# A short convolution moved to TensorE, a filter transpose moved through DRAM, and a new load order, in a long-convolution and MLP kernel

## The chip, the cores and the metric

The kernel runs on one core of one Trainium2 chip. The metric is the device time of an execution in microseconds (us). Executions agree within about 1%. PE is TensorE, DVE is VectorE, ACT is ScalarE, POOL is GpSimd and SP is SyncE, which issues most of the transfers. The granted clock is the share of its full speed that PE was given, as the profile records it. The matmuls of this kernel write to buffers in PSUM; the copy of a result from there into SBUF, by ACT or DVE, is called an eviction here.

## The reference

All inputs are bf16. S = 2048 tokens, D = 512 channels, F = 1376, four taps in the short convolution.

```python
def _A_ref(q, k, v, shift_k, ssm_k, ssm_D):
    k_shift = sum(k_pad[:, t:t+S, :] * shift_k[:, ks-1-t] for t in range(4))   # short causal convolution
    kv = k_shift * v
    y = irfft(rfft(kv, 2*S) * rfft(ssm_k, 2*S))[:S] + kv * ssm_D               # long causal convolution
    return q * y
def _B_ref(x, w1, b1, w2, b2):
    return gelu(layernorm(x) @ w1 + b1) @ w2 + b2
x = A_q
x = x + _A_ref(layernorm(x), ...);  x = x + _B_ref(layernorm(x), ...)
x = x + _A_ref(layernorm(x), ...);  x = x + _B_ref(layernorm(x), ...)
```

(The text is shortened: casts and padding are left out, and the loop over taps is written as a sum.) Both A layers use the same k, v and filter, so y is the same in both. The kernel computes it once, in a first part, and then runs four groups of tokens twice through the MLP part.

## The kernel before

The long convolution is a transform in two stages of matmuls: stage 1 with table F, a transpose, stage 2 with table W, a product with the transformed filter, then the inverse with table M, a transpose, and the last stage with table G. Filter and data both go through stage 1 and a DVE transpose. The parts that the change touches:

```python
# loads: k and its 3-token halo, the filter on ACT's queue, v and the tables on SP's
nc.sync.dma_start(kh[:, KS - 1:, :], k_d.rearrange(TOK, p=P))
for p0, n in ((1, 112), (113, 15)):
    nc.scalar.dma_start(kh[p0:p0 + n, 0:h, :], ...)
for ct in range(CT):
    nc.scalar.dma_start(Kraw[:, ct, :], A_ssm_k[ct * P:(ct + 1) * P, :])
nc.sync.dma_start(uv[:], v_d.rearrange(TOK, p=P))
# ... cut ...
def kv_chunk(cc):                       # short convolution and product with v, on DVE, 128 channels
    nc.vector.tensor_tensor(m[:], kh[:, h:h + NT, c0:c0 + CW], sb(0), ALU.mult)
    for t in range(1, KS):
        nc.vector.tensor_tensor(m2[:], kh[:, h - t:h - t + NT, c0:c0 + CW], sb(t), ALU.mult)
        nc.vector.tensor_tensor(m[:], m[:], m2[:], ALU.add)
    nc.vector.tensor_tensor(uv[:, :, c0:c0 + CW], m[:], uv[:, :, c0:c0 + CW], ALU.mult)
# ... cut ...
def stage1(src, dst, cc, tag):          # for the filter (Ktok to ZK) and for the data (uv to ZX)
    for q in range(4):
        for i in range(8):
            nc.tensor.matmul(pz[:, i, :], Ft[:, q // 2, :], src[:, tau, c0:c0 + CW], start=True, stop=True)
        nc.scalar.activation(ZT[:, 8 * q:8 * q + 8, :], pz[:], AF.Copy)
    nc.vector.transpose(dst[...], ZT[...])          # as 32-bit pairs, 128x2048
# ... cut ...
k_transpose()
for cc in range(NCH):
    kv_chunk(cc)
    stage1(Ktok, ZK, cc, "pa")
    stage1(uv, ZX, cc, "pb")
```

After this come stage 2 of the filter (with swapped half copies made by DMA), the product loop (`x_mul`, `x_inv`), four bare transposes and the last stage. A layernorm of token group 0 is placed in the loop.

## Time and profile before

| | before |
|---|---|
| time, median of 4 runs | 340.0 us (339.73 to 340.84) |
| span of the profiled execution | 338.0 us |
| mean granted PE clock | 0.884 |
| DVE busy, PE busy | 225.2 us, 244.7 us |
| end of the first part (first DVE product of the output) | 158.66 us |

The prediction below shows the lines: the chain of work that ended last, the chain in order of time, the busy time by stretch, and the groups. A busy time is a sum over an engine and says nothing about order. The chain says which engine's work the next work waited for. The windows tell, for one stretch, how full each engine was; where one engine is nearly full, its work is the first candidate for what sets the length of the stretch.

### The profile page before, as it was taken

The page shows a single profiled execution, that of the slowest core. Times are in us where ns is not written, and L with a number is a line of the kernel's source. Part 1 is how long each engine was busy: PE and PEld are TensorE (multiplying, and loading weights), DVE is VectorE, ACT ScalarE, POOL GpSimd, SP SyncE. Part 2 cuts the span into 40 slices and gives each one's busy share as a digit, 9 for nine tenths or more (in the row PEclk, how much of TensorE's full clock was granted, in tenths as well). Part 3 has the DMA queues.
Part 4 walks back from the last instruction along what each step waited for, and adds up shares of the span by engine and source line. Part 5 has one row for each costly group of instructions (what it writes and reads, how often), then busy time and mean ns, then how long its engine had stood idle before and what let it go on. Part 6 is the DMA issues. An engine that isn't in the chain of part 4 may idle for free.

```text
span 338.0 us, 3487 instructions
## 1 busy us (share of the span) xinstructions
PE 244.7 (72%) x1312; PEld 122.5 (36%) x1312; DVE 225.2 (67%) x361; ACT 164.3 (49%) x206; POOL 19.8 (6%) x26
## 2 busy tenths in 40 slices
PE   0007546253786997107599999989999999999995
PEld 0007536153321322002235444444444444444442
DVE  2208999999534999894987988888787682020122
ACT  0106878055778887004667736246271653726300
POOL 3000000000010000001112112101011110000000
PEclk9999967555578999656969999999999999999999
DMA  7990000006599445000000000000000001010011
GB/s 229 374 390 4 2 0 2 0 0 249 186 234 222 106 167 167 0 0 0 2 0 1 2 0 0 2 0 1 3 0 0 2 0 50 14 45 17 18 62 47
DMA packets 7040, 21.94 MB, mean 65 GB/s; under 512 B 912, under 2 KB 4593, under 8 KB 5872
## 3 DMA queue, kind: packets, MB, share of 16 engines
q1 hardware_dynamic: 5890, 19.14, 18.1%
q10 hardware_dynamic: 1022, 2.59, 2.1%
q8 instruction: 10, 0.16, 0.2%
q0 software_dynamic: 112, 0.00, 0.1%
q14 instruction: 6, 0.05, 0.1%
HBM read 15.44 MB, written 2.10 MB: 52 GB/s over the span
## 4 chain that ended last, share of the span: by engine, by line
DVE 46%; PE 36%; DMA 8%; ACT 5%; POOL 3%; issue 2%; DVEq 0%; POOLq 0%; ACTq 0%
PE po L328 17%; PE ph L316 14%; DVE arena L200 9%; DMA arena<-in_A_ssm_k_dram 6%; DVE st L169 6%; DVE arena L266 5%; DVE kvm L159 4%; DVE kvt L158 4%; DVE arena L177 4%; ACT arena L207 3%; POOL rs L173 3%; DVE T L235 3%; DVE arena L244 3%; DVE T L234 2%; DMA arena<-in_A_k_dram 2%; DVE arena L297 2%
## 5 line engine op out<-in xcount | busy, mean ns | idle before, releaser
L328 PE MATMUL po<-arena 128*128 128x512 bf16 (+1 forms) x352 | 80.7, 379 | 1.3 <-DVE arena L331 1.3
L316 PE MATMUL ph<-arena 128*128 128x512 bf16 (+1 forms) x352 | 79.6, 387 | 0.7 <-ACT arena L308 0.7
L318 ACT ACTIVATE arena<-ph,B 128x512 bf16<-128x512 f32 (+1 forms) x88 | 60.2, 687 | 29.5 <-PE ph L316 29.5
L331 DVE TENSOR_TENSOR arena<-po,arena 128x512 bf16<-128x512 f32 x32 | 21.9, 683 | 50.1 <-PE po L328 50.1
L316 PEld LDWEIGHTS <-arena 128*128 128x128 bf16 (+1 forms) x352 | 35.9, 102 | 43.3 <-issue 3.9
L328 PEld LDWEIGHTS <-arena 128*128 128x128 bf16 (+1 forms) x352 | 33.8, 98 | 38.8 <-issue 1.4
L169 DVE BATCH_NORM_STATS2 st<-arena 128x6 f32<-128x512 bf16 x64 | 42.4, 676 | 5.2 <-DMA arena<-in_A_q_dram 4.5
L198 PE MATMUL pz<-arena,Ft 128*128 128x128 bf16 x256 | 25.8, 275 | 27.1 <-DVE arena L160 16.7
L199 ACT ACTIVATE ZT<-pz 128x1024 bf16<-128x1024 f32 x32 | 30.6, 1033 | 22.2 <-PE pz L198 21.7
L308 ACT ACTIVATE arena<-pt 128x512 bf16<-128x512 bf16 x32 | 17.3, 594 | 42.8 <-PE pt L307 42.5
L198 PEld LDWEIGHTS <-Ft 128*128 128x128 bf16 x256 | 22.6, 127 | 30.6 <-issue 26.3
L200 DVE STREAM_TRANSPOSE arena<-ZT 128x2048 f32<-128x2048 f32 x8 | 29.4, 3671 | 3.0 <-ACT ZT L199 3.0
L173 POOL TENSOR_TENSOR rs<-rs,mhalf 128x4 f32<-128x4 f32 x16 | 16.1, 1009 | 202.8 <-DVE rs L172 202.8
L187 PE MATMUL pk<-IDt,arena 128*128 128x128 bf16 x64 | 6.5, 285 | 26.9 <-DVE arena L143 26.6
L273 PE MATMUL py<-arena,Gt 128*128 128x512 bf16 x32 | 9.6, 452 | 17.9 <-DVE arena L266 17.6
L177 DVE TENSOR_SCALAR arena<-arena,rs,nm 128x512 bf16<-128x512 bf16 x64 | 22.1, 407 | 0.6
L242 PE MATMUL pv<-T,arena 128*128 128x512 bf16 x64 | 18.7, 393 | 3.0 <-DVE T L234 1.5
L274 ACT ACTIVATE arena<-py 128x1024 bf16<-128x1024 f32 x8 | 7.9, 1023 | 22.0 <-PE py L273 22.0
L232 ACT ACTIVATE xb<-px 128x1024 bf16<-128x1024 f32 x16 | 16.3, 1040 | 3.4 <-DVE T L235 3.3
L207 ACT ACTIVATE arena<-pk 128x1024 bf16<-128x1024 f32 x16 | 15.1, 1058 | 2.6 <-PE pk L206 2.6
L266 DVE STREAM_TRANSPOSE arena<-arena 128x2048 f32<-128x2048 f32 x4 | 16.2, 4121 | 0.1
L189 ACT ACTIVATE arena<-pk 128x2048 bf16<-128x2048 bf16 x4 | 7.3, 1874 | 18.4 <-PE pk L187 18.4
(38 smaller groups left out, 189.5 us busy)
## 6 DMA issues: line engine op xcount, KB each, us to landing
arena<-arena SPq DMA_DIRECT2D x8, 512.0 KB, 7.1
arena<-in_A_k_dram SPq DMA_DIRECT2D x1, 2048.0 KB, 12.5
arena<-in_A_ssm_k_dram ACTq DMA_DIRECT2D x4, 512.0 KB, 19.5
arena<-in_A_v_dram SPq DMA_DIRECT2D x1, 2048.0 KB, 12.8
arena<-tabM SPq DMA_DIRECT2D x1, 2048.0 KB, 7.6
arena<-in_A_q_dram SPq DMA_DIRECT2D x1, 2048.0 KB, 9.2
out_dram<-arena SPq DMA_DIRECT2D x16, 128.0 KB, 1.7
arena<-in_B_w_dram SPq DMA_DIRECT2D x1, 1376.0 KB, 5.9
```

The costliest lines, as they stand in the source:

```text
L169: nc.vector.bn_stats(st[:, i, :], x_t[:, GT * g + i, :])
L173: nc.gpsimd.tensor_tensor(rs[:], rs[:], mhalf[:], ALU.pow)
L177: nc.vector.tensor_scalar(out=dst[:, i, :], in0=x_t[:, GT * g + i, :], scalar1=rs[:, i:i + 1], scalar2=nm[:, i:i + 1], op0=ALU.mult, op1=A ...
L198: nc.tensor.matmul(pz[:, i, :], Ft[:, q // 2, :], src[:, tau, c0:c0 + CW], start=True, stop=True)
L199: nc.scalar.activation(ZT[:, 8 * q:8 * q + 8, :], pz[:], AF.Copy)
L200: nc.vector.transpose(dst[:, :, c0:c0 + CW].bitcast(F32).rearrange("p k c -> p c k"), ZT[:].bitcast(F32).rearrange("p b c -> p c b"))
L207: nc.scalar.activation(ZK[:, 2 * j:2 * j + 2, :], pk[:], AF.Copy)
L266: nc.vector.transpose(V2[:, :, c0:c0 + CW].bitcast(F32).rearrange("p k c -> p c k"), ZX[:, :, c0:c0 + CW].bitcast(F32).rearrange("p b c -> ...
L316: nc.tensor.matmul(ph[0:m, :], W1t[:, ct, ft * P:ft * P + m], lt[:, ct, :], start=ct == 0, stop=ct == CT - 1)
L318: nc.scalar.activation(ht[0:m, ft, :], ph[0:m, :], AF.Gelu_apprx_tanh, bias=B1[0:m, ft:ft + 1])
L328: nc.tensor.matmul(po[:], ht[0:m, ft, i * P:(i + 1) * P], W2t[0:m, ft, :], start=ft == 0, stop=ft == FT - 1)
L331: nc.vector.tensor_tensor(xs, po[:], xs, ALU.add)
```

## The change

The intent is to take work off DVE in the first part. The short convolution becomes matmuls with diagonal matrices, accumulated in PSUM over the four taps, so that DVE only multiplies by v. The filter's transpose after stage 1 goes to DRAM and back by DMA. The filter is loaded first. Evictions from PSUM are shared between ACT and DVE, PSUM buffers rotate over four instead of two and two, and the product loop lags by two steps instead of one. The core of the diff:

```diff
-    nc.sync.dma_start(kh[:, KS - 1:, :], k_d.rearrange(TOK, p=P))
     for ct in range(CT):
-        nc.scalar.dma_start(Kraw[:, ct, :], A_ssm_k[ct * P:(ct + 1) * P, :])
+        nc.sync.dma_start(Kraw[:, ct, :], A_ssm_k[ct * P:(ct + 1) * P, :])
+    for t4 in range(4):
+        nc.sync.dma_start(kn[:, 4 * t4:4 * t4 + 4, :], k_d.rearrange(TOK, p=P)[:, 4 * t4:4 * t4 + 4, :])
     nc.sync.dma_start(uv[:], v_d.rearrange(TOK, p=P))
 ... cut: tables, constants ...
+    for ct in range(CT):
+        for t in range(KS):
+            nc.gpsimd.tensor_scalar(out=DG[:, ct, t, :], in0=IDt[:], scalar1=sF[:, ct, t:t + 1], ...)
-    def kv_chunk(cc):        # 8 DVE instructions for each 128 channels
 ... cut ...
+        def k_filter_stage1(q):
+            for i2 in range(4):
+                for i in range(2):
+                    nc.tensor.matmul(pz[:, i, :], Ft[:, q // 2, :], Ktok[:, tau, :], start=True, stop=True)
+                evac(E_S1K[q][i2], ZT[:, 2 * i2:2 * i2 + 2, :], pz[:])
+            nc.sync.dma_start(apf(Zd, 8 * q * P * D, [[D, P], [P * D, 8], [1, D]]), ZT[:])
+        def kv_transpose(t4):     # k to channel-major, 16 PE transposes and one DVE copy
 ... cut ...
+        def kv(ct, o):
+            for i in range(8):
+                for t in range(KS):
+                    nc.tensor.matmul(pu[:, i, :], w, DG[:, ct, t, :], start=t == 0, stop=t == KS - 1)
+            nc.vector.tensor_tensor(us, pu[:], us, ALU.mult)
 ... cut ...
+        for q in range(4):
+            k_filter_stage1(q)
+            kv_transpose(q)
+        for k0 in range(0, NA, 8):
+            for g in range(4):
+                nc.sync.dma_start(ZK[32 * g:32 * g + 32, k0:k0 + 8, :],
+                                  apf(Zd, (32 * g + k0) * D, [[P * D, 32], [1, 8 * D]]))
+        for cc in range(4):
+            for o in range(2):
+                kv(cc, o)
+            if cc > 0:
+                stage1(cc - 1)
 ... cut: stage 2, the loop with a lag of two, the tail ...
```

## The prediction

(The text is cut, with marks, where it rested on figures that no trace or run of this case shows. The sums stand as they were: none of the terms of the 314 us is cut, but terms of three sums beside it are. In step (2) the 4.25 us for a quarter were chosen and not summed, and what DVE needs for its copies is cut beside them. The trip through DRAM came to 53 us; with the trace's numbers alone it is the same, as an estimate: 1 MB at 374 GB/s is 2.8 us, 4.2 MB are 11.2, each with the 1.7 us in which 128 KB landed: 35.5 + 17.4 = 52.9. In the cross-check the added work came to 29.2 us and the net to 25. In the trace before, the granted clock was 1.00 in the first of the two bursts and 0.50 in the second, and in the stretches it was 0.67, 0.84 and 0.94 with PE busy 35.9 of 65.8, 9.8 of 13.8 and 25.5 of 31.6 us.)

> **What bounds the kernel now.** I began with the page's chain that ended last, because a share of busy time averages over stages with different limits. Its first line splits the span by engine:
>
> ```profile
> DVE 46%; PE 36%; DMA 8%; ACT 5%; POOL 3%; issue 2%; DVEq 0%; POOLq 0%; ACTq 0%
> ```
>
> The same chain in order of time gives the stages. In these lines the columns are start, duration (us), what:
>
> ```profile
> 6.97 19.28 DMA arena<-in_A_ssm_k_dram
> 26.50 1.12 DVE kvt L158
> ...
> 95.94 10.19 ACT arena L207 x11
> ...
> 137.76 16.20 DVE arena L266 x4
> ...
> 158.66 1.24 DVE arena L297
> ```
>
> Nothing but loading happens until 26.5 us. From 26.5 to 92.3 the chain is VectorE alone (short convolution L155 to L160, transposes L200). From 92.3 to 106.1 it is mostly ScalarE evicting the filter's second stage. From 106.1 to 137.7 it is the VectorE-paced product loop, then 16.2 us of four bare transposes. The MLP part starts with L297 at 158.66. The diff touches nothing after that line, so I cut the run there and asked for the busy time of each engine by stretch:
>
> ```profile
> 0.00:26.50 26.50, 0.00 (x0) 0.00 (x0) 4.62 (x8) 1.28 (x1) 2.68 (x8) 1.00 0.89 318
> 26.50:92.30 65.80, 35.85 (x328) 29.77 (x329) 62.69 (x39) 41.34 (x40) 0.00 (x0) 0.67 0.15 52
> 92.30:106.10 13.80, 9.76 (x28) 3.19 (x28) 4.54 (x14) 11.41 (x14) 1.04 (x1) 0.84 0.93 239
> 106.10:137.70 31.60, 25.47 (x92) 8.33 (x92) 28.59 (x40) 23.59 (x25) 0.00 (x0) 0.94 0.52 143
> ```
>
> Columns: stretch, length, busy PE, PEld, DVE, ACT, POOL, granted clock, DMA share, GB/s. In the second row DVE is busy 62.7 of 65.8 us while DMA is used 15%: that row is what the change attacks. The costs come from the groups:
>
> ```profile
> L200 DVE STREAM_TRANSPOSE arena<-ZT 128x2048 f32<-128x2048 f32 x8 | 29.4, 3671 | 3.0 <-ACT ZT L199 3.0
> L159 DVE TENSOR_TENSOR kvm<-kvm,kvt 128x2048 bf16<-128x2048 bf16 x12 | 14.4, 1209 | 0.1
> L158 DVE TENSOR_TENSOR kvt<-arena,SK 128x2048 bf16<-128x2048 bf16 x12 | 14.2, 1213 | 0.0
> L244 DVE CAST arena<-pv 128x1024 bf16<-128x1024 f32 x8 | 9.8, 1219 | 0.9 <-PE pv L242 0.9
> L207 ACT ACTIVATE arena<-pk 128x1024 bf16<-128x1024 f32 x16 | 15.1, 1058 | 2.6 <-PE pk L206 2.6
> ```
>
> And two bursts of 128-column matmuls from the timeline show PE's two speeds, 61 ns each (1.95/32) and 110 ns each (4.42/40):
>
> ```profile
> 36.76 1.95 PE L198 MATMUL pz<-arena,Ft 128*128 128x128 bf16 x32 [2.05 <-DVE arena L160]
> 50.66 4.42 PE L198 MATMUL pz<-arena,Ft 128*128 128x128 bf16 x40 [1.56 <-DVE arena L160]
> ```
>
> [...]2048 elements in SBUF take 1.21 us, 1024 f32 elements from PSUM take 1.22. The trace has no DVE copy of bf16 from PSUM; [...]the stretch's granted clock of 0.67 goes with PE busy half the time. [...]the 32 KB identity on ACT's queue landed 12.7 us after its issue[...], and the filter[...] landed 17.9 to 20.5 us after issue. [...]the stores of 128 KB here landed in 1.7.
>
> **The change part by part.**
>
> (1) Load order. The filter (2.1 MB) is now first on SP's queue, ahead of k, v and the tables. The page shows 229 GB/s in the first slice (8.45 us, 1.9 MB) and 374 in the next. The remaining 0.3 MB then takes about 1 us, plus landing: 10.5 us instead of 26.5. A tiny add with D, whose load took until 9.3 us, precedes PE, and the b1 cast waited until 13.6 on the same in-order DVE. I choose PE's start at 12 us.
>
> (2) Filter path. 64 transposes took 6.5 us of PE; they stay, their evictions move to DVE[...], so PE is through at 18.5. Stage 1 becomes 32 matmuls of 512 columns, with 64 more transposes for k. Per quarter: PE 8 x 0.22 + 16 x 0.1 = 3.4 us, ACT 3 x 1.03 = 3.1[...]. Four rotating PSUM buffers make this a chain; I choose 4.25 per quarter, 17 in all: 35.5 us. The four filter transposes on DVE (4 x 3.67 = 14.7) are gone; 4.2 MB goes to DRAM and back instead. At the last quarter, [...]home at about 53 us.
>
> (3) Short convolution on PE. 28 TENSOR_TENSORs at 1.21 and one 1.23 copy leave DVE (35 us); four products (4.8) become eight from PSUM at 1.22 (9.8). PE gains 256 matmuls of 128 columns, beside 128 of stage 1: 384 x 0.061 = 23.4 us at full clock, 42 at half. DVE has 9.8 + 14.7 = 24.5, ACT 16 x 1.03 = 16.5. PE is dense from 12 us on, so I expect nearly full clock and PE and DVE to pace each other: 24.5 plus about 4.5 for the hand-overs of a 3.67 us transpose against 1.22 us products: 29 us, to 64.5.
>
> (4) Filter stage 2. It needs the DRAM data (53) and PSUM in rotation, so it starts at 64.5. ACT owes four evictions (4.1) and then 12 of 16 (12.4); DVE takes 4. That is 16 us: 80.5. The layernorm of group 0 fits in here, if q arrives: its buffer is free at 64.5, and 9.2 us from issue to landing gives 74.
>
> (5) Product loop. Same matmuls, same two products per step, same alternating evictions; only the lag is deeper. It is already 28.6 of 31.6 us DVE-busy, so I give it 31: 111.5.
>
> (6) Tail. Last transposes and the first output block: 158.66 - 137.7 = 21 us, unchanged: 132.5. The MLP then starts 158.66 - 132.5 = 26 us earlier. 340 - 26 = 314 us.
>
> A cross-check by DVE work: removed 35 + 4.8 + 14.7 = 54.5, added 9.8 (products)[...] + 9.8 (eight evictions) = 29.2; net 25 us. The earlier start adds 14 and the new hand-overs take back about as much.
>
> **The rivals.** First, PE becomes the bound of the convolution at the low clock. For: clock 0.67 in that stretch before, and 3.67 us transposes can stall PE. Against: PE has twice the work there. It would make (3) 42 to 45 us: 327 to 330. Second, the product loop waits for its table M or for q, both issued late on SP behind the eight half-swap copies. For: the diff places these loads after stage 2, where they were spread before. Against: in the trace before, q's load was issued at 87.54 although the code names it after the swaps, first issued at 92.55, so the order follows readiness; M's buffer is free at about 36. If it fails, about 8 to 12 us are lost: 322 to 326. Third, the DRAM round trip is slower than I think[...], and stage 2 waits. It has 11 us in hand, so it must take almost twice as long to cost anything; 317 to 320. Fourth, an upside: PE starts at 10.5, hand-overs are hidden, stage 2 is shared so well that ACT is free: 304 to 307.
>
> **Range and chances.** The sum is 314. The errors are mostly one-sided waits of up to 16 us and an upside of 10, and they are unlikely to come all together: 303 to 327. To be within 2% it would have to end above 333, which takes the low clock and a late load both; slower has no mechanism I can see, as at least 25 us of DVE work goes.
>
> **What would show it.** Right: first PE work at 10 to 14 us; filter stage 1 over by about 36; eight PSUM products of about 1.2 us[...] on DVE; granted clock above 0.85 from 36 to 65; stage 2's first matmul waiting on PSUM or ACT, not on DMA; the product loop still at about 3.5 us per two steps; the MLP stretch at 179 us, starting near 132. Wrong: [...]convolution matmuls at 110 ns; PE waiting for M or DVE for q after 80 us; stage 2 waiting on the reads from DRAM. If the MLP stretch itself changes, my cut at L297 was wrong.

## The result and the profile after

| | before | after |
|---|---|---|
| median | 340.49 us (16 runs, 338.9 to 341.33) | 309.65 us (11 runs, 308.67 to 311.49) |
| profiled span | 338.0 us | 306.8 us |
| mean granted PE clock | 0.884 | 0.939 |
| DVE busy, PE busy | 225.2, 244.7 us | 202.7, 248.8 us |
| end of the first part | 158.66 us | 127.11 us |

The ratio is 0.9098, with a 95% interval of 0.9078 to 0.9119. A ratio here is the mean time of one kernel's runs over that of the other's in the same rounds, so it is not quite the ratio of the medians that are quoted. The prediction was 314 us with 303 to 327: the time lies in the range, 4.3 us under the 314.

The chain that ended last, by engine, and then five pieces of the same chain in order of time (start, duration, what):

```profile
PE 43%; DVE 38%; DMA 5%; issue 5%; ACT 4%; POOL 3%; SPq 0%; DVEq 0%; ACTq 0%; POOLq 0%
```

```profile
2.13 8.47 DMA arena<-in_A_ssm_k_dram
...
30.57 6.54 PE p L227 x114
37.11 1.93 PE p L238 x32
...
42.15 4.19 DVE arena L240
...
127.11 1.24 DVE arena L370
```

DVE's share fell from 46% to 38% and PE's rose from 36% to 43%. Where before DVE stood in the chain from 26.5 to 92.3 us, all but alone (the chain has about 3 us of PE and ACT at 85.6), now PE's convolution (L227), PE's stage 1 (L238) and DVE's transposes (L240) take turns. The line L370 at 127.11 answers to L297 at 158.66: the first part ends 31.55 us earlier.

The busy time by stretch, with the same columns as in the prediction (stretch, length, busy PE, PEld, DVE, ACT, POOL, granted clock, DMA share, GB/s). The rows are loading, the filter's stage 1, the convolution, the filter's stage 2, the product loop, the tail, and the MLP part:

```profile
0.00:10.64 10.64, 1.63 (x9) 0.89 (x9) 0.35 (x3) 0.00 (x0) 2.81 (x8) 1.00 0.79 246
10.64:30.57 19.93, 17.28 (x166) 12.50 (x166) 14.31 (x13) 12.78 (x13) 9.50 (x17) 1.00 1.04 395
30.57:58.35 27.78, 23.41 (x371) 22.54 (x371) 18.71 (x11) 12.50 (x14) 0.00 (x0) 0.94 1.01 270
58.35:70.99 12.64, 8.56 (x33) 3.08 (x32) 11.27 (x6) 12.02 (x14) 0.00 (x0) 1.00 0.52 120
70.99:104.87 33.88, 23.98 (x96) 9.21 (x96) 31.83 (x50) 24.52 (x26) 0.00 (x0) 0.98 0.78 227
104.87:127.11 22.24, 4.66 (x12) 1.58 (x12) 17.53 (x9) 2.05 (x2) 2.02 (x3) 0.50 0.00 0
127.11:306.80 179.69, 169.28 (x854) 80.20 (x852) 108.74 (x258) 84.46 (x127) 15.10 (x15) 0.97 0.04 13
```

No engine is full between 10.64 and 58.35 us. PE is the fullest (17.3 of 19.9, then 23.4 of 27.8) and its clock is granted at 0.94 or more, where the stretch before had 0.67. The product loop is again nearly all DVE (31.8 of 33.9). The MLP part is 179.7 us against 338.0 - 158.66 = 179.3 before, so the whole gain is in the first part.

The groups of the new work (busy us, mean ns of one, then the idle time before it):

```profile
L240 DVE STREAM_TRANSPOSE arena<-ZT 128x2048 f32<-128x2048 f32 x4 | 17.0, 4245 | 1.8 <-ACT ZT L172 1.8
L229 DVE TENSOR_TENSOR arena<-p,arena 128x1024 bf16<-128x1024 f32 x8 | 9.7, 1220 | 7.3 <-PE p L227 7.3
L174 DVE COPY arena<-p 128x2048 bf16<-128x2048 bf16 x8 | 9.5, 1222 | 4.6 <-PE p L218 2.5 <-PE p L201 2.0
L227 PE MATMUL p<-DG,arena 128*128 128x128 bf16 x256 | 16.8, 231 | 0.9 <-DVE arena L174 0.6 <-ACT ZT L172 0.3
```

The products from PSUM took 1.22 us each, the duration that the prediction used, and so did the bf16 copies of 2048 elements from PSUM. (A matmul's mean of 231 ns is the duration of overlapping instructions; 16.8 us of busy time over 256 is 66 ns, and the chain's 6.54 us over 114 is 57.) The four transposes left in L240 took 4.25 us each, where the same shape took 3.67 before; no run settles why.

Two lines of the timeline answer the prediction's open questions on late data: when the transfer of q was issued, and when the layernorm's statistics of group 0 ran:

```profile
75.95 1.24 SPq L318 DMA_DIRECT2D arena<-in_A_q_dram  x1
...
99.78 1.28 DVE L183 BATCH_NORM_STATS2 st<-arena 128x6 f32<-128x512 bf16 x2
```

The transfer of q landed 15.1 us after its issue, at about 91 us. The layernorm's first part ran at the end of the product loop and not in stage 2, and its last part between the transposes of the tail.

One more line of the timeline shows what stage 2's first matmul waited for, and one window shows the transfers just after it began:

```profile
58.35 0.59 PE L248 MATMUL p<-arena,Wt 128*128 128x512 bf16 x2 [0.31 <-ACT ZT L172]
```

```profile
61.00:63.80 2.80, 2.05 (x8) 0.77 (x8) 2.80 (x3) 2.80 (x5) 0.00 (x0) 1.00 0.00 0
```

It waited 0.31 us, and for ACT's eviction; no later matmul of stage 2 waited for a transfer either. The transfers (the last reads of the filter from DRAM among them) ended only at about 61 us: from 61.0 to 63.8 there are 0 GB/s.

### The profile page after: what moved, and what is told of

Its sections match the earlier page's. It is cut to its first block, busy times and chain, and to the rows that moved or that the text cites. A ratio compares the mean times of both kernels' runs of the same rounds, so it can differ in the third digit from the quotient of the medians.

```text
span 306.8 us, 4006 instructions
## 1 busy us (share of the span) xinstructions
PE 248.8 (81%) x1536; PEld 130.0 (42%) x1536; DVE 202.7 (66%) x348; ACT 148.3 (48%) x194; POOL 29.4 (10%) x43
## 4 chain that ended last, share of the span: by engine, by line
PE 43%; DVE 38%; DMA 5%; issue 5%; ACT 4%; POOL 3%; SPq 0%; DVEq 0%; ACTq 0%; POOLq 0%
PE po L401 19%; PE ph L389 15%; DVE st L183 7%; DVE arena L174 5%; DVE arena L191 4%; DVE arena L281 4%; DVE ZT L265 3%; DVE arena L240 3%; PE p L227 3%; POOL rs L187 3%; DMA arena<-in_A_ssm_k_dram 3%; DVE ZT L264 3%; DMA Zd<-ZT 2%; DVE arena L370 2%; DVE arena L371 2%
## 5 line engine op out<-in xcount | busy, mean ns | idle before, releaser
L401 PEld LDWEIGHTS <-arena 128*128 128x128 bf16 (+1 forms) x352 | 33.9, 98 | 38.6 <-issue 1.2
L183 DVE BATCH_NORM_STATS2 st<-arena 128x6 f32<-128x512 bf16 x64 | 42.3, 676 | 0.7
L172 ACT ACTIVATE arena<-p 128x1024 bf16<-128x1024 f32 x28 | 27.3, 1062 | 27.9 <-PE p L289 24.9
L381 ACT ACTIVATE arena<-pt 128x512 bf16<-128x512 bf16 x32 | 17.3, 594 | 43.1 <-PE pt L380 39.4
L172 ACT ACTIVATE ZT<-p 128x1024 bf16<-128x1024 f32 x28 | 26.7, 1027 | 18.8 <-PE p L238 14.2
L289 PE MATMUL p<-arena,Gt 128*128 128x512 bf16 x32 | 9.4, 466 | 21.7 <-DVE arena L281 21.7
L274 PE MATMUL p<-ZT,arena 128*128 128x512 bf16 x64 | 16.5, 378 | 3.9 <-DVE arena L174 3.4
L240 DVE STREAM_TRANSPOSE arena<-ZT 128x2048 f32<-128x2048 f32 x4 | 17.0, 4245 | 1.8 <-ACT ZT L172 1.8
L172 ACT ACTIVATE xb<-p 128x1024 bf16<-128x1024 f32 x16 | 16.2, 1061 | 2.7 <-DVE ZT L265 2.6
L227 PE MATMUL p<-DG,arena 128*128 128x128 bf16 x256 | 16.8, 231 | 0.9 <-DVE arena L174 0.6
L227 PEld LDWEIGHTS <-arena 128*128 128x128 bf16 x256 | 16.1, 105 | 1.2 <-DVE arena L174 0.8
L281 DVE STREAM_TRANSPOSE arena<-arena 128x2048 f32<-128x2048 f32 x4 | 16.4, 4156 | 0.0
L380 PE MATMUL pt<-IDt,arena 128*128 128x128 bf16 x128 | 11.7, 229 | 4.8 <-DVE arena L191 4.1
L174 DVE CAST arena<-p 128x1024 bf16<-128x1024 f32 x12 | 14.6, 1217 | 1.4 <-PE p L248 1.4
## 6 DMA issues: line engine op xcount, KB each, us to landing
arena<-in_A_q_dram SPq DMA_DIRECT2D x1, 2048.0 KB, 15.1
```

What stands on the lines that cost most here:

```text
L172: nc.scalar.activation(dst, src, AF.Copy)
L174: nc.vector.tensor_copy(dst, src)
L183: nc.vector.bn_stats(st[:, i, :], x_t[:, GT * g + i, :])
L227: nc.tensor.matmul(pu[:, i, :], w, DG[:, ct, t, :], start=t == 0, stop=t == KS - 1)
L240: nc.vector.transpose(ZX[:, :, c0:c0 + CW].bitcast(F32).rearrange("p k c -> p c k"), ZT[:].bitcast(F32).rearrange("p b c -> p c b"))
L281: nc.vector.transpose(V2[:, :, c0:c0 + CW].bitcast(F32).rearrange("p k c -> p c k"), ZX[:, :, c0:c0 + CW].bitcast(F32).rearrange("p b c -> ...
```

## The experiments

The theory was: three parts of the change each bring about a third (the load order, the filter's way through DRAM, the convolution on PE), each because it takes a stretch off DVE or off the wait in front of it. The rivals were that one of them is hidden behind another and brings nothing, that the load order alone did it, and, for the convolution, that PE or DVE alone paces it now. Unless the kernel before or the run before is named, an experiment edits the kernel after. A difference "to after" is that of the medians, 309.65 us for after. All outputs were correct, but for one run that was wrong on purpose.

### Undoing the load order

```diff
+    for ct in range(CT):
+        nc.scalar.dma_start(Kraw[:, ct, :], A_ssm_k[ct * P:(ct + 1) * P, :])
     nc.scalar.dma_start(Ft[:], F_h.ap().bitcast(BF16))
-    for ct in range(CT):
-        nc.sync.dma_start(Kraw[:, ct, :], A_ssm_k[ct * P:(ct + 1) * P, :])
```

> The changed kernel with the filter's four loads put back on ACT's queue behind the identity, as before the change. If the early filter is part of the gain: the filter lands near 20 to 26 us instead of 10.6, PE's dense work starts that much later, and as PSUM is handed round in program order nothing can fill the gap: 10 to 15 us longer than the changed kernel, 320 to 325 us. Rival (later waits absorb the start): under 4 us longer, 310 to 314.

Measured: 318.48 us, ratio 0.9364 (0.9317 to 0.9411), 8.8 us more than after. The chain in time shows the load:

```profile
4.51 16.68 DMA arena<-in_A_ssm_k_dram
```

The filter was there at 21.2 us instead of 10.6. Of this 10.6 us delay 8.8 reached the end, so most of it was on the path, and nothing filled the gap: PE was busy 1.6 of the first 21.2 us. That is less than the 10 to 15 us expected and far more than the rival's 4.

### The load order alone, in the kernel before

```diff
+    for ct in range(CT):
+        nc.sync.dma_start(Kraw[:, ct, :], A_ssm_k[ct * P:(ct + 1) * P, :])
     nc.sync.dma_start(SKr[:], apf(A_shift_k, 0, [[0, P], [1, D * KS]]))
 ...
-    for ct in range(CT):
-        nc.scalar.dma_start(Kraw[:, ct, :], A_ssm_k[ct * P:(ct + 1) * P, :])
```

> The kernel before with the filter's loads first on SP's queue and nothing else changed. The filter lands near 11 us, k near 17, and DVE, which idled from 16 to 26 us for the filter, runs from 17 on: 6 to 8 us shorter than before, ratio 0.977 to 0.982. Rival (k lands so much later that the start is only shifted): within 1%.

Measured: 330.93 us, ratio 0.9737 (0.9698 to 0.9775), against 339.97 for before in the same rounds: 9.0 us less. DVE's timeline shows its first product of the short convolution:

```profile
18.39 1.23 DVE L155 TENSOR_TENSOR kvm<-arena,SK 128x2048 bf16<-128x2048 bf16 x1 [3.74 <-DMA arena<-in_A_k_dram]
```

It starts at 18.4 us and waits for k, not for the filter. The gain is a little more than the 6 to 8 us expected. What the late filter had cost in the kernel before is one line of its timeline:

```profile
26.33 0.18 DVE L143 TENSOR_TENSOR arena<-arena,Dc 128x4 bf16<-128x4 bf16 x1 [10.20 <-DMA arena<-in_A_ssm_k_dram]
```

DVE had begun its products at 13.77 us, and after two of them it stood 10.2 us at this add of 0.18 us, which needs the filter; the next product ran right behind it, at 26.41. So an obvious rival is untested: to place the add further back in DVE's order might bring a part of these 9 us without any new load order. The load order as it was changed is worth about 9 us in either kernel: with the DVE-bound stretch behind it and with the new one. It is a third of the whole and not all of it.

### The filter's transpose back on DVE

```diff
-        def k_filter_stage1(q):
+        def k_filter_stage1(cc):
 ... 128-column matmuls, as stage1 has them ...
-            nc.sync.dma_start(apf(Zd, 8 * q * P * D, [[D, P], [P * D, 8], [1, D]]), ZT[:])
+            nc.vector.transpose(ZK[:, :, c0:c0 + CW].bitcast(F32).rearrange("p k c -> p c k"), ZT...)
-        for k0 in range(0, NA, 8): ... the 16 reads from DRAM
```

> The changed kernel with the filter's stage 1 transposed by VectorE again, no trip through DRAM (four transposes of about 4.2 us added on DVE, same evictions, same PE columns). If DVE paces the stretch from 11 to 58 us (it has 14 us idle there): 8 to 14 us longer, 318 to 324. Rival (the 9 to 14 us that DVE idles there, waiting for PE, swallow the transposes): under 3 us longer, 309 to 313; then the trip through DRAM bought nothing.

Measured: 320.28 us, ratio 0.9426 (0.9382 to 0.947), 10.6 us more than after. The window of this stretch:

```profile
10.60:43.90 33.30, 25.83 (x304) 24.75 (x305) 30.34 (x17) 13.14 (x13) 9.55 (x17) 0.85 0.54 211
```

DVE is busy 30.3 of 33.3 us. Four transposes of 4.25 us are 17.0 us of DVE work, of which 10.6 reached the end; that the rest went into the gaps that DVE has in the kernel after is likely but not shown.

### The convolution back on DVE, in three steps

The first version undid the convolution and nothing else:

```diff
-            for o in range(2):
-                kv(cc, o)
+            kv_chunk(cc)
```

(with the halo load, the broadcast taps and the buffers of the kernel before; no kv_transpose and no diagonals).

> The changed kernel with the short convolution back on VectorE (28 more products and sums of 1.2 us, eight PSUM products and four PSUM copies of k fewer), everything else as changed. If the convolution on PE is the largest part: DVE has about 55 us of work in place of 28 in that stretch, 20 to 26 us longer, 330 to 336. Rival (PE was the bound of the new stretch, so giving it back 15 us of matmuls and 4 us of transposes pays for half): 8 to 14 us longer, 318 to 324.

Measured: 339.88 us, ratio 1.0007 (0.9969 to 1.0044): 30.2 us more than after, the whole gain. That is too much, as the other two parts were still in. The chain in time shows why:

```profile
93.44 1.32 SPq L247
94.81 14.63 DMA arena<-tabM
```

Table M lies in the buffer from which DVE now reads k to the last. Its load was issued behind the swapped half copies, at 94.8 us, and the chain stands 14.6 us for it. So this run mixed two things. In the second version the load of M stands in front of stage 2:

```diff
+        nc.sync.dma_start(Mt[:], M_h.ap().bitcast(BF16))
         for j in range(NA // 2):
             k_stage2(j)
-        nc.sync.dma_start(Mt[:], M_h.ap().bitcast(BF16))
```

> The last run's kernel (convolution on VectorE) with one thing more: the load of table M is written before the filter's second stage, so that it is issued as soon as the convolution has done with k's buffer (about 71 us) and not behind the swaps at 94.8, where the last run's chain waited 14.6 us for it. Theory: of the 30 us that the last run lost, some 10 to 13 were this wait and the convolution itself is 17 to 20: 327 to 330 us. Rival (the convolution's place alone is worth the 30 us, the wait hides other work): within 3 us of 340.

Measured: 327.57 us, ratio 0.9611 (0.9592 to 0.963): 17.9 us more than after, and 12.3 less than with the late table. But this version still has the evictions on DVE that the change moved there because DVE had become free. The third version gives those of the filter's transposes and stage 1 back to ACT, as the kernel before had them:

```diff
-        E_KT, E_kT = "DDDD", "DDDD"
-        E_S1K = ["ADAA", "ADAA", "ADAA", "ADAA"]
+        E_KT, E_kT = "AAAA", "AAAA"
+        E_S1K = ["AAAA", "AAAA", "AAAA", "AAAA"]
```

> The kernel with the convolution on VectorE and table M early (327.6 us), with the filter's eight DVE evictions (9.7 us) given back to ScalarE. Its DVE was busy 52 of 53 us from 21 to 74. If the three parts add to more than the whole because the trip through DRAM was paid for with evictions on DVE, which cost nothing only while the convolution is not there: 7 to 10 us shorter, 318 to 321. Rival (PE or the filter's chain bounds it as well): within 3 us of 327.6.

Measured: 322.45 us, ratio 0.9476 (0.9445 to 0.9507): 5.1 us less than the second version, between what the two sides expected. The windows of the second and of the third version:

```profile
21.00:74.00 53.00, 16.54 (x126) 12.27 (x125) 52.12 (x39) 20.41 (x22) 0.00 (x0) 0.69 0.76 229
```

```profile
21.00:74.00 53.00, 24.19 (x166) 15.10 (x166) 48.00 (x34) 32.14 (x36) 0.00 (x0) 0.68 0.78 228
```

With the convolution on DVE that engine is busy 52.1 and 48.0 of 53 us, and PE's granted clock falls to 0.69 and 0.68, the 0.67 of the kernel before. So the convolution on PE is worth 12.8 us against the fairest version, 17.9 against the one with the evictions left as they are. With the fairest, the three parts undone one at a time cost 8.8 + 10.6 + 12.8 = 32.2 us; the whole change is 340.49 - 309.65 = 30.8. With this version they are nearly additive (with the second the sum is 37.3), and none is hidden behind another. The rotation over four PSUM buffers and the lag of two steps were not undone by themselves; this sum leaves little for them, and no run shows it.

### What paces the convolution now: two taps instead of four

This kernel gives a wrong result (two taps of four). It takes half of the convolution's matmuls away and leaves DVE's work as it is.

```diff
-                for t in range(KS):
+                for t in range(2):
-                    nc.tensor.matmul(pu[:, i, :], w, DG[:, ct, t, :], start=t == 0, stop=t == KS - 1)
+                    nc.tensor.matmul(pu[:, i, :], w, DG[:, ct, t, :], start=t == 0, stop=t == 1)
```

> The changed kernel with two of the four taps left out, a wrong result on purpose: 128 of 256 convolution matmuls go, 7.5 us of PE at 58 ns each; DVE and ACT keep all their work. If PE paces the stretch from 31 to 58 us (busy 23.4 of 27.8 us): 5 to 7.5 us shorter, 302 to 305. If the hand-overs to DVE do (18.7 busy, each convolution tile waits for a product, each transpose blocks two): 0 to 2.5 us shorter, 307 to 310. If both in turn, as I predicted: 2.5 to 5.

Measured: 304.94 us, ratio 0.8945 (0.8906 to 0.8983), 4.7 us less than after. The stretch's window:

```profile
30.57:53.70 23.13, 18.21 (x252) 16.35 (x254) 20.98 (x12) 15.27 (x17) 0.00 (x0) 0.93 1.01 281
```

The stretch is 23.1 us instead of 27.8. The 128 matmuls that went are 128 x 57 ns = 7.3 us of PE. If PE alone paced it, all 7.3 would have come; if DVE alone did, none. So PE paces the larger part of it, and with half of PE's convolution gone DVE is next: it is busy 21.0 of 23.1 us. The four runs lie between 303.6 and 306.0 us, so the split is rough.

### The sharing of stage 2's evictions

```diff
-        E_K2 = "AADA"
+        E_K2 = "AAAA"
```

> The changed kernel with all 16 evictions of the filter's second stage on ScalarE, as before the change, in place of 12. If ScalarE's sum paces that stage: 4 x 1.03 = 3 to 4 us longer, 312.5 to 314. Rival (the stage waits as long for the evictions that DVE is late with, behind two 4.2 us transposes): within 1.5 us of 309.7.

Measured: 311.51 us, ratio 0.9143 (0.9114 to 0.9172). That is 1.9 us more than after by the medians, and the interval touches that of after (up to 0.9119). The result lies between what the two sides expected, and the time does not decide between them. The trace says a little more: ACT's last eviction of stage 2 ends at 75.7 us instead of 72.8, about 3 us later, as its four more evictions of 1 us would have it, and not all of this reached the end. At most a small part of the gain is in this sharing.

### The layernorm of group 0 early

The prediction put this layernorm into stage 2, and q came too late for it. Here the first group of q is loaded early on ACT's queue, into the place of k's first transposed quarter (free after the first chunk), and the layernorm is placed behind the third chunk of the convolution.

```diff
+            if cc == 0:
+                q0 = place("q0", [P, GT, D], 132 * K)
+                nc.scalar.dma_start(q0, q_d.rearrange(TOK, p=P)[:, 0:GT, :])
 ...
+            if cc == 2:
+                layernorm(lna0, 0, q0)
 ...
-            if j == 3:
-                layernorm(lna0, 0)
```

> The changed kernel with group 0 of q loaded by itself on ACT's queue into the place of k's first transposed quarter, and its layernorm (5.8 us of DVE) done between the convolution's products, where DVE idles 9 us, in place of the end of the product loop. Theory (it is on the path where it is now): 2 to 4.5 us shorter, 305 to 308. Rival (it delays the products and so PE by as much): within 1.5 us of 309.7.

Measured: 317.5 us, ratio 0.9315 (0.9293 to 0.9336): 7.9 us more than after. Neither side had expected this. DVE's and PE's timelines:

```profile
46.43 1.29 DVE L184 BATCH_NORM_STATS2 st<-arena 128x6 f32<-128x512 bf16 x2 [9.64 <-DMA arena<-in_A_q_dram]
```

```profile
48.90 1.01 PE L239 MATMUL p<-arena,Ft 128*128 128x128 bf16 x8 [9.75 <-DVE arena L230]
```

The 0.5 MB of q took 12.6 us to land, while M (13.1 us from issue to landing) and the reads of the DRAM trip (9.1 us, the median) were under way. In DVE's order the statistics stood in front of the next product: DVE waited 9.6 us for q, and PE 9.8 us for DVE. Here a layernorm placed ahead of its data cost more than one that ran late.

### Half of the last transposes through DRAM

The tail of 22 us holds four bare transposes on DVE (16.4 us). Here the right half of the columns goes to DRAM and back, as the filter does, and DVE transposes only the left half.

```diff
+        def inv_store(k0):
+            nc.sync.dma_start(apf(Yd, k0 * P * HC, [[HC, P], [P * HC, 8], [1, HC]]), ZX[:, k0:k0 + 8, HC:D])
+        def inv_load(k0):
+            for g in range(4):
+                nc.sync.dma_start(V2h[1][32 * g:32 * g + 32, k0:k0 + 8, :],
+                                  apf(Yd, (32 * g + k0) * HC, [[P * HC, 32], [1, 8 * HC]]))
-        for cc in range(4):
+        for cc in range(2):
             inv_transpose(cc)
```

(The store follows each fourth `x_inv`; the last stage runs in halves of 256 columns.)

> A candidate that goes on from the changed kernel: after the product loop, VectorE transposes only the left 256 columns (two transposes, 8.2 us in place of 16.4); the right 256 go through DRAM as the filter does, stored in four parts while the loop still runs and read back in 16 pieces at its end. From this case's transfers (1 MB parts to DRAM landed in 5.5 to 7.7 us, the 4.2 MB read back took about 19 us beside M's load) I estimate 4 us for the last store of 0.5 MB and 8 for the 2.1 MB read, so the first output block starts about 13 us after the loop's last eviction, not 22: 7 to 10 us shorter, 300 to 303. Rival (the stores and reads of 512-byte rows are slow or stand behind the weights on SP's queue): 0 to 3 us shorter, 307 to 310.

Measured: 310.01 us, ratio 0.9118 (0.906 to 0.9177): no change to after. The stores landed in 3.7 us and the reads in 4.2 (medians). The first output block came at 122.43 us instead of 127.11, 4.7 us earlier, but the MLP part then took 185.8 us instead of 179.7: PE waited 5.7 us there for a residual sum of DVE:

```profile
170.41 1.01 PE L420 MATMUL po<-arena 128*128 128x512 bf16 x2 [5.67 <-DVE arena L423]
```

In DVE's order that sum (L423) stood behind a whole layernorm. The gain was made and given back.

### The same, with the layernorm behind the transposes

```diff
-            step(j, 0, 512, "AD"[j % 2])
-            if j == 3:
-                layernorm(lna0, 0)
+            step(j, 0, 512, "AAD"[j % 3])
 ...
             inv_transpose(cc)
+        layernorm(lna0, 0)
```

> The candidate above with two things more: group 0's layernorm is written after the two transposes, where DVE would wait for the right half anyway, and five of the loop's 16 evictions are DVE's instead of eight (DVE then has 24.8 us in the loop, ScalarE 28). 2 to 5 us shorter than the candidate above. Rival (ScalarE becomes the loop's pace and the layernorm the first block's): within 1 us of it, or longer.

The edit also leaves one in three of the loop's evictions to DVE instead of one in two. Measured: 304.47 us, ratio 0.8951 (0.8923 to 0.8979), 5.2 us less than after and 5.5 less than the run before it, a little more than the 2 to 5 expected. The run does not separate the two. The first output block came at 116.49 us, 10.6 us earlier than in after, but the MLP part was 186.7 us long. The timeline has the issue of the 16 reads on SP's queue, and PE's wait in the MLP part:

```profile
104.51 10.51 SPq L285 DMA_DIRECT2D arena<-Yd  x16
...
164.45 1.01 PE L419 MATMUL po<-arena 128*128 128x512 bf16 x2 [6.46 <-DVE arena L422]
```

Two things were left: the 10.5 us in which the reads are issued, and the residual sum (L422), which stands behind a layernorm in DVE's order. (PE's granted clock from 98 to 121 us was 0.73.)

### The reads on two queues

```diff
-                nc.sync.dma_start(V2h[1][32 * g:32 * g + 32, k0:k0 + 8, :],
+                q = nc.sync if g % 2 else nc.scalar
+                q.dma_start(V2h[1][32 * g:32 * g + 32, k0:k0 + 8, :],
 ...
-            for half in range(2):
-                for t in (t0, t0 + 4):
-                    inv_stage2(t, half)
+            for t in (t0, t0 + 4):
+                for half in range(2):
+                    inv_stage2(t, half, "AD"[half] if t < 4 else "A")
```

> The last candidate but with the 16 pieces of the right half read back on two queues (half on SP's, half on ACT's), since their issue alone took 10.5 us on SP's; the blocks are done left and right in turn, and the first block's right half is evicted by DVE. Issue then takes about 5.3 us on each, the last piece lands some 4 us earlier, the first block starts 2 to 3 us earlier: 301.5 to 303 us. Rival (the first block waited for PE's cold matmuls and not for the pieces): within 1 us of 304.5.

Measured in five rounds: 297.76 us (296.8 to 298.87), ratio 0.8755 (0.8728 to 0.8782). It beats both kernels: 42.3 us less than before in the same rounds (340.08), 11.9 less than after. But the reason that had been given for it fell. The timeline:

```profile
103.65 9.88 SPq L286 DMA_DIRECT2D arena<-Yd  x8
...
103.67 9.61 ACTq L286 DMA_DIRECT2D arena<-Yd  x8
...
116.48 1.23 DVE L389 TENSOR_TENSOR arena<-arena 128x2048 bf16<-128x2048 bf16 x1
...
157.36 0.59 PE L420 MATMUL po<-arena 128*128 128x512 bf16 x2 [0.15 <-DVE arena L423]
```

The waits of SP's own queue (what waited for what: us in total, times, longest):

```profile
SPq L286 <- DMA arena<-Yd: 6.2, 1, 6.2
```

Half as many reads on each of two queues still took 9.9 and 9.6 us to issue, almost as long as 16 on one. One of the issuing instructions takes about 0.39 us, eight are 3.1 us; 6.2 us of SP's stretch are a wait for earlier reads to land; whether the program or the queues set this wait is not shown. The first output block came at 116.48, the same as in the run before. All of the further 6.7 us is in the MLP part, 179.2 us instead of 186.7: PE's wait for the residual sum is 0.15 us instead of 6.46 (a later one is 2.4), and its granted clock from 160 to 180 us is 1.00 instead of 0.83. In DVE's order the sum now stands in front of that layernorm (it runs at 156.7 us; at 163.8 in the run before). So the cost of the two runs before goes with DVE's order. Since the first block did not move, the queues did not bring the first block earlier; that the new order of the last stage or its one eviction on DVE changed DVE's order is what remains of the edit, and no run separates these two. Nor does the run show that two queues are worth nothing, as ACT paid for its reads:

```profile
113.33 1.94 ACT L173 ACTIVATE arena<-p 128x1024 bf16<-128x1024 f32 x2 [13.50 <-DMA arena<-Yd]
```

ACT's first eviction of the last stage stood behind the reads that ACT issues itself, and came at 113.3 us; in the run before it came at 110.9.

## Why the prediction was right

Its steps, with the lengths that the windows show:

| step | predicted, us | measured, us | error |
|---|---|---|---|
| (1) load order, to PE's dense start | 12 | 10.64 | -1.4 |
| (2) filter path | 23.5 | 19.93 | -3.6 |
| (3) convolution on PE | 29 | 27.78 | -1.2 |
| (4) filter stage 2 | 16 | 12.64 | -3.4 |
| (5) product loop | 31 | 33.88 | +2.9 |
| (6) tail | 21 | 22.24 | +1.2 |
| sum | 132.5 | 127.11 | -5.4 |

(The errors are rounded from the windows' lengths; the sum is that of the unrounded ones.)

The mechanism held. DVE lost the convolution and four transposes, the filter came first, and the end of the first part moved by 31.55 us. The errors are sizes of terms.

Step (1): right in kind. The estimate of 10.5 us for the filter's landing was right (10.60; the rest after the first slice was 0.2 MB and not 0.3, which changes nothing). The 1.5 us that were added for the small add with D were not needed: it ran at 10.72 us, when nine of PE's transposes were already done. The two runs on the load order price the step at about 9 us each, not at the 14 us that the cross-check gave the earlier start (measured by the windows, PE's start moved by 15.9).

Step (2): mis-sized. The filter's transposes took 5.2 us from PE's start instead of 6.5. The prediction allowed 4.25 us for a quarter. The first three took 2.87 us each (k's transposes begin at 18.04, 20.91 and 23.77); the fourth also waited 1.8 us for a buffer that the store to DRAM still held. Hand-overs cost less than was put down. The home-coming of the DRAM data, put at 53 us, was at about 61: its reads were issued from 35.5 us on, behind M's 2 MB (30.4). It cost nothing, because stage 2's first matmul waited for ACT only. The prediction's third rival therefore happened in part and was hidden. (With 11 us in hand on the 17.5 from 35.5 to 53, the trip had to take 1.6 times as long to cost anything, not almost twice.)

Step (3): right in length (29 against 27.8) and in clock (above 0.85; it was 0.94). The first rival, PE at the low clock, did not come. The run with two taps shows that PE and DVE share the pace, as the step said. But the length is in part luck. The sum was 24.5 us of DVE's work and 4.5 of hand-overs; in this window DVE is busy 18.7 us and idle 9.1, because most of the third transpose and all of the fourth (from 57.41 and 62.54 us) ran behind its end. PE, busy 23.4 us as predicted, stands nearer to the pace. The sizes were off as well: the matmuls took 57 ns and not 61, and the transposes 4.25 us and not 3.67, so that over the whole run DVE lost 22.5 us of work and not the 25 of the cross-check. The diagonal matrices, which the prediction did not count, were made by POOL within the 9.5 us that the second window shows it busy, beside other work.

Step (4): mis-sized, and one part of it wrong. The step counted 16.5 us of ACT's work and was left with 16; ACT did 14 evictions and was busy 12.0 of 12.6 us. That it is mostly ACT's stretch was right, though PE waited once, 1.7 us, for an eviction that DVE made behind its last transpose. The length depends on the cut: 70.99 us is the loop's first matmul, but in the kernel before the stage was cut where ACT passes to the loop's first eviction (106.1), and that is at 72.6 here. Cut there, step (4) is 14.2 us and step (5) 32.3, and their errors are -1.8 and +1.3. That "the layernorm of group 0 fits in here, if q arrives" failed in its condition: q was issued at 75.95 us, not as soon as its buffer was free (64.5 in the prediction; in the trace its last reader, stage 1, ended at 58.0). The prediction had taken from the trace before that the order follows readiness, since q's load had been issued ahead of the half copies there. In the kernel after it stood behind them; why, no run shows.

Steps (5) and (6): the place of the layernorm is the likely cause, but no run isolates it. In the kernel before it lay in the stage-2 stretch (DVE busy 4.5 us there). Now its statistics lie in the product loop, where DVE, the fullest engine, is busy 31.8 us instead of 28.6; from the like cut at 72.6 us it is 31.1 of 32.3, so a part of the added work went into gaps that the loop had before (3 us of 31.6). Its last part of 1.4 us stands between the tail's transposes, and 1.2 us is the error there. The second rival, a late M or q, is met here too: M was early, q was late, and it cost at most the 4 us by which these two steps are over, not the 8 to 12 of a full wait. Whether an early q would have gained these is not shown: the one run that tried it placed the layernorm too early and lost 7.9.

So the first four steps came out 9.5 us shorter than predicted, and the last two took back 4.1 of these (7.9 and 2.5 with the like cut): the first part ended 5.4 us early by the profile, 4.3 by the medians. The MLP part was unchanged, as the cut at L297 assumed.

## What to carry to other kernels

Undo each part of a change by itself, and give back what the other parts took from it (a buffer that a later load needs, an eviction moved to the freed engine): the same part cost 30, 18 and 13 us in three versions here. When a stage's end moves and the total does not, look for the wait that has appeared in the next stage: here DVE had an instruction that PE waited for behind one that was not needed yet, and in the run in which that order came out otherwise 6.7 us went, while the transfers that were thought to be the limit took almost as long as before. A small instruction can hold an engine as long as a large one if its data are late (here an add of 0.18 us held DVE for 10.2): look for it in front of the first dense work. A transfer may be slower than planned and cost nothing (here the filter's came home at about 61 us and not at 53), so ask first who waits for it.
